# Laying out the on-chip memory of a fused attention and expert kernel anew, and splitting the products of its last layer by halves

## The chip, the cores and the metric

The kernel runs on one core of a Trainium2 chip. The metric is the time of one execution on the device in microseconds (us), the median of several runs. The engines of a core work side by side: TensorE (PE) multiplies, VectorE (DVE), ScalarE (ACT) and GpSimd (POOL) work on elements, SyncE (SP) issues the transfers (DMA).

## The reference, cut to what matters

```python
x = attention(q, k, v)                                     # block-causal softmax, 4 x 8 heads of 64
h = np.maximum(np.maximum(x @ w1, x @ w2), x @ w3)         # 2304 tokens, 512 -> 768
x = h @ w_out                                              # 768 -> 512
p = domain_probs / (domain_probs.sum(-1, keepdims=True) + 1e-09)
out = np.zeros((N, D))
for e in range(4):                                         # 512 -> 1024 -> 512
    h = np.maximum(x @ w1[e], 0.0)
    out += p[:, e:e + 1] * (h @ w2[e])
```

The change concerns the loop over the four experts alone.

## The kernel before, in words

**Arithmetic.** Every matrix product is made of fp32r parts: an operand is split into a high part (a cast on ACT) and a low part (the operand less its high part, a subtraction on DVE), and three matmuls, high by high, high by low and low by high, stand for one. The expert layers add a recursive scheme: the operands are cut into quarters, seven combinations of them (`b11`, `b21`, `t1` to `t4`, `b22`) are multiplied, and sums of the seven products give the four quarters of the result.

**Passes.** The tokens go through the experts in three passes (`NPASS`, line 626; pass 0, 1 and 2 in the code). A pass takes 768 tokens as two columns of `CT` = 384. In pass 0 the second layer is done directly (`second`, line 916, six output tiles of twelve matmuls for each half of an expert). In passes 1 and 2 it is done with the seven combinations (`second_mixed`, line 1043): `sides` (line 963) makes of each combination of the hidden quarters a high and a low part, 768 wide and for each of two halves of the hidden units; `product2` (line 993) multiplies it by the combined weights, twelve matmuls for each of two output halves `d`; and the product is added to running sums `accs`.

**First layer.** `hidden2` (line 855) does the first layer for one of four groups of hidden units: seven products of six matmuls in three PSUM tiles, in the order `b11 t2 t1 b21 t3 b22 t4`, with additions on DVE between them (`plus`), and the hidden quarters written by `put`: in passes 1 and 2 to `hq` tiles (`Mixed`, line 944). Between its products it takes steps of two generators: `between`, the second layer of the expert before (`pend`), and `behind`, which makes the operands of the next pass.

**Weights.** The combined weights of the first layer are kept in DRAM and loaded by `weights_in` (line 812) into a ring of two tiles `w1` (1792 KB each); a load waits until the last product that reads the old tile is done. Pass 1 begins with the expert that pass 0 ended with, so its first two groups use the two tiles that are there (`kept_w`). The combined weights of the second layer (1024 KB each) are loaded by `wide2` (line 984) into a ring of two tiles `w2`.

**Places.** Pass 0 has a pool `p2` (line 1102) with its weights `w2`, `ws`, `raw`, `mix`, its hidden values `hh` and `hl` and temporaries `tmp`. It is closed at line 1158, and so is the pool of the `arena` (line 54; attention's results, and the output sums of pass 0 and the input of pass 1). Pool `p3` (line 1160) takes over their memory for passes 1 and 2: `accs`, `w2`, `hx`, `tmp`, `pb`, `hq`. A tile of `p3` may be written when the readers of what lay there before are done.

**Last expert.** The second layer of the last expert of pass 2 has no work behind it. `second_last` (line 1006) runs the seven combinations in the order `THEN` (line 684), leaves sums that share an accumulator in PSUM, and stores the four output quarters as they are complete.

**Order.** The kernel is written in program order; a scheduler at build time moves instructions of an engine ahead of others by a model of their times, program order being the priority. `keep_in_program_order` takes an instruction out of that: it stays behind what stands before it. In `second_last` every DVE instruction is kept so (`kept`, line 1007).

Of the kernel before, what the change touches and what calls it, by code (L numbers as in the profile page):

```python
# [23 lines left out]
def program(tc, q, k, v, w123, w_out, probs, e_w1, e_w2, out):  # L24
# [27 lines left out]
    wide = ExitStack()  # L52
    big = wide.enter_context(tc.tile_pool(name="big", bufs=1))
# [15 lines left out]
    mp = moe.enter_context(tc.tile_pool(name="moe", bufs=1))  # L69
    hidden = [mp.tile([P, NF, S], F32R, name=x, tag=x) for x in ("hh", "hl")]  # L70
# [668 lines left out]
    def mix():  # L739

        def put(name, src):
            t = tile_in(p3, "hx", [P, 2, 2 * CT], F32R, 4)
# [83 lines left out]
    def weights_out(e, n):  # L826
        w = tile_in(p2, "w2", W2_, F32R, 3)
        s = tile_in(p2, "ws", W2_, F32R)
        raw = tile_in(p2, "raw", [P, 4, QW_], F32)
        nc.sync.dma_start(out=raw, in_=e_w2[e, n])  # L830
        mix_ = tile_in(p2, "mix", [P, 4, QW_], F32)
# [23 lines left out]
    def hidden2(w, xc, pool, put, between, behind, held_back):  # L855
# [8 lines left out]
        def plus(name, x, y):  # L864
            t = put.room(name) if name[0] == "c" else tile_in(pool, "tmp", [P, CT], F32, NTMP)
# [4 lines left out]
        q1 = tile_in(pool, "tmp", [P, CT], F32, NTMP)  # L870
# [18 lines left out]
    class Plain:  # L889
# [11 lines left out]
        def room(self, name):  # L901
            return tile_in(p2, "tmp", [P, CT], F32, NTMP)
# [6 lines left out]
    def paced(it, wait):  # L909
        for _ in range(wait):  # L910
            yield
        for _ in it:
            yield
            yield

    def second(p, e, hs, wo, first_, last):
        for c in range(2):
            for t in range(TPC):
# [5 lines left out]
                for i in range(G):  # L924
# [3 lines left out]
                    nc.tensor.matmul(out=o, lhsT=hh[:, ts], rhs=wh, start=i == 0, stop=False)  # L928
# [34 lines left out]
    def sides(hs, room, less=None):  # L963
        less = less or (lambda out_, x, y, op: nc.vector.tensor_tensor(out_, x, y, op=op))  # L964

        todo = dict(
            b11=(0, ()), b21=(2, ()), t1=(0, (0, 1, 0)), t2=(0, (0, 3, 0)), t3=(1, (1, 3, 1)), b22=(3, ()),
            t4=(0, (0, 2, 0)),
        )
        for name in THEN:  # L970
            n, mix_ = todo[name]
            made = []
            for h in hs:
                if mix_:
                    x, y, z = mix_
                    less(h[:, x], h[:, y], h[:, z], ALU.subtract)
                src = h[:, n].rearrange("x j s -> x (j s)")
                t = room()
                nc.scalar.copy(t[:, 0], src)  # L979
                less(t[:, 1], src, f(t[:, 0]), ALU.subtract)  # L980
                made.append(t)
                yield made

    def wide2(e, name, pool=None, tag="w2"):
        w = tile_in(pool or p3, tag, [P, NPR, 2, QW_], F32R, 2)
# [7 lines left out]
    def product2(o, w, hx, order, d, start, stop):  # L993
        for n, i in enumerate(order):
            wh, wl = (w[:, i, x, d * P:(d + 1) * P] for x in range(2))
            xh, xl = (hx[n // 2][:, x, (n % 2) * CT:(n % 2 + 1) * CT] for x in range(2))
            for m, (a, b) in enumerate(((wh, xh), (wh, xl), (wl, xh))):
                nc.tensor.matmul(  # L998
                    out=o, lhsT=a, rhs=b, start=start and n == 0 and m == 0, stop=stop and n == NPR - 1 and m == 2,
                    skip_group_check=True,  # L1000
                )

    def ring():
        return tile_in(p3, "hx", [P, 2, 2 * CT], F32R, 4)

    def second_last(p, e, hs, order, accs):
        def kept(out_, x, y, op):
            tc.keep_in_program_order(nc.vector.tensor_tensor(out_, x, y, op=op))

        names = iter(FIRST * 2)  # L1010
        prepared = sides(hs, lambda: xc_tile(next(names)).rearrange("x n k s -> x n (k s)"), kept)
        made = [next(prepared) for _ in range(4)][1::2]
# [5 lines left out]
        ends = dict(b21=(0, 0), t3=(1, 1), b22=(0, 1), t4=(1, 0))  # L1018
        q1 = [None, None]
        for n, name in enumerate(THEN):  # L1020
            w = wide2(e, name, *((xp, "w1") if n % 2 == 0 else (p3, "w2")))
            hx = made.pop(0)
            for d in range(2):
                x = next(prepared, None)
                if d and x:
                    made.append(x)
                m, a = ms[d][chain[name]], accs[d]
                product2(m, w, hx, order, d, name in ("b11", "t1", "t2"), name in ("b21", "b22", "t4"))
                if name == "b11":
                    q1[d] = tile_in(p3, "tmp", [P, CT], F32, NTMP)  # L1030
                    nc.scalar.copy(q1[d], m)
                    yield
                    continue
                x = dict(t1="t1", t2="b22", b22="t4").get(name)
                if x:
                    kept(a[x], a[x], q1[d], ALU.add)
                x = into[name]
                kept(a[x], a[x], m, ALU.add)
                if name in ends:
                    store(p, d, *ends[name], a[x])  # L1040
                yield

    def second_mixed(p, e, hs, order, accs, first_, last):
        prepared = sides(hs, ring)
# [217 lines left out]
```

## Time and profile before

| | us |
|---|---|
| median of 3 runs | 1267.93 |
| lowest, highest | 1266.81, 1269.63 |
| the profiled execution, its own time | 1269.37 |
| its span, first to last instruction | 1267.3 |
| PE busy in the span | 1212.8 |
| mean granted TensorE clock | 0.988 |

The profile is of one execution. A time in its rows counts from the span's start. Attention and the two layers after it fill the span to about 520 us, pass 0 of the experts goes on to about 776 us, and passes 1 and 2 to the end. [...]

### The profile page before, as it was taken

The page shows a single profiled execution, that of the slowest core. Times are in us where ns is not written, and L with a number is a line of the kernel's source. Part 1 is how long each engine was busy: PE and PEld are TensorE (multiplying, and loading weights), DVE is VectorE, ACT ScalarE, POOL GpSimd, SP SyncE. Part 2 cuts the span into 40 slices and gives each one's busy share as a digit, 9 for nine tenths or more (in the row PEclk, how much of TensorE's full clock was granted, in tenths as well). Part 3 has the DMA queues.
Part 4 walks back from the last instruction along what each step waited for, and adds up shares of the span by engine and source line. Part 5 has one row for each costly group of instructions (what it writes and reads, how often), then busy time and mean ns, then how long its engine had stood idle before and what let it go on. Part 6 is the DMA issues. An engine that isn't in the chain of part 4 may idle for free.

```text
span 1267.3 us, 19648 instructions
## 1 busy us (share of the span) xinstructions
PE 1212.8 (96%) x7353; PEld 1162.2 (92%) x7353; DVE 938.4 (74%) x1780; ACT 514.9 (41%) x1076; POOL 355.6 (28%) x442
## 2 busy tenths in 40 slices
PE   6789998999999999999999998999999999999997
PEld 5669997999999999989999997999999999999996
DVE  7969899667566644468988894668787887677866
ACT  7876778445444421333434340233322223222221
POOL 4958787454154122333333340000000000000000
PEclk9989999999999999999999999999999999999998
DMA  8655574654533486678888855777887877767653
GB/s 314 239 166 185 171 260 159 190 165 148 158 101 117 143 322 225 235 295 309 319 302 295 314 204 168 276 279 283 349 301 293 306 264 270 271 248 267 230 205 110
DMA packets 82643, 299.67 MB, mean 236 GB/s; under 512 B 8748, under 2 KB 18036, under 8 KB 69492
## 3 DMA queue, kind: packets, MB, share of 16 engines
q1 hardware_dynamic: 82548, 298.42, 66.7%
q8 instruction: 58, 0.95, 0.3%
q14 instruction: 37, 0.30, 0.1%
HBM read 215.26 MB, written 83.14 MB: 235 GB/s over the span
## 4 chain that ended last, share of the span: by engine, by line
PE 81%; DVE 7%; ACT 6%; DMA 2%; issue 2%; POOL 1%; SPq 0%; ACTq 0%; DVEq 0%; POOLq 0%
PE m L846 27%; PE m L492 18%; PE o L998 16%; PE o L928 3%; PE o L929 3%; PE o L930 3%; PE st L181 3%; PE pv L346 2%; PE m L998 2%; PE tt L251 2%; ACT p L202 2%; DVE mn L195 1%; PE pv L305 1%; DMA w<-ka 1%; DVE arena L426 1%
## 5 line engine op out<-in xcount | busy, mean ns | idle before, releaser
L492 PE MATMUL m<-xh,wt 128*128 128x288 f32 x1120 | 236.7, 297 | 2.1 <-DVE mt L530 1.4
L846 PE MATMUL m<-t,w 128*128 128x384 f32 x1152 | 229.5, 338 | 0.0
L998 PE MATMUL o<-hx,w 128*128 128x384 f32 x1176 | 226.0, 337 | 0.0
L998 PEld LDWEIGHTS o<-hx,w 128*128 128x128 f32 x1176 | 208.1, 188 | 0.0
L846 PEld LDWEIGHTS m<-t,w 128*128 128x128 f32 x1152 | 205.1, 189 | 1.9
L492 PEld LDWEIGHTS m<-xh,wt 128*128 128x128 f32 x1120 | 183.1, 188 | 3.3 <-DVE mt L530 1.8
L846 PE MATMUL m<-b,w 128*128 128x384 f32 x864 | 176.8, 339 | 6.2 <-DMA w<-ka 6.2
L979 ACT CAST hx<-hq 128x768 fp32r<-128x768 f32 x98 | 81.6, 837 | 218.7 <-PE o L998 150.0
L492 PE MATMUL m<-xl,wt 128*128 128x288 f32 x560 | 164.8, 294 | 0.0
L846 PEld LDWEIGHTS m<-b,w 128*128 128x128 f32 x864 | 154.3, 189 | 9.4 <-DMA w<-ka 6.5
L964 DVE TENSOR_TENSOR hx<-hq,hx 128x768 fp32r<-128x768 f32 x98 | 93.3, 954 | 39.7 <-ACT hx L979 39.4
L213 POOL TENSOR_SCALAR p<-p,sm 128x128 f32<-128x128 f32 (+1 forms) x144 | 99.4, 706 | 33.6 <-DVE sm L211 27.9
L492 PEld LDWEIGHTS m<-xl,wt 128*128 128x128 f32 x560 | 105.2, 188 | 0.3
L866 DVE TENSOR_TENSOR tmp<-m,tmp 128x384 f32<-128x384 f32 x144 | 77.9, 549 | 24.8 <-PE m L846 24.3
L202 ACT ACTIVATE p<-st,mn 128x128 f32<-128x128 f32 (+3 forms) x144 | 78.7, 558 | 16.1 <-DVE mn L195 15.8
L492 PE MATMUL m<-hh,wo 128*128 128x288 f32 x384 | 81.4, 298 | 2.7 <-ACT arena L541 1.3
L181 PE MATMUL st<-kk,q 128*128 128x128 f32 (+3 forms) x336 | 67.0, 333 | 10.6 <-ACT q L126 5.3
L928 PE MATMUL o<-w,hh 128*128 128x512 f32 x192 | 74.7, 391 | 0.7 <-ACT hh L906 0.5
L929 PE MATMUL o<-w,hh 128*128 128x512 f32 x192 | 74.7, 390 | 0.0
L930 PE MATMUL o<-w,hl 128*128 128x512 f32 x192 | 74.0, 390 | 0.0
L800 POOL TENSOR_TENSOR w<-raw,w 128x512 fp32r<-128x512 f32 x32 | 47.9, 1517 | 89.8 <-ACT w L798 70.8
L866 DVE TENSOR_TENSOR hq<-m,tmp 128x384 f32<-128x384 f32 x96 | 52.7, 553 | 25.0 <-PE m L846 24.4
(153 smaller groups left out, 2076.7 us busy)
## 6 DMA issues: line engine op xcount, KB each, us to landing
w<-kb SPq DMA_DIRECT2D x56, 1024.0 KB, 5.0
w<-ka SPq DMA_DIRECT2D x30, 1792.0 KB, 7.4
ka<-w SPq DMA_DIRECT2D x16, 1792.0 KB, 6.7
wt<-held SPq DMA_DIRECT2D x54, 512.0 KB, 4.1
kb<-ws SPq DMA_DIRECT2D x16, 1024.0 KB, 7.1
kb<-w SPq DMA_DIRECT2D x16, 768.0 KB, 4.6
arena<-in_w SPq DMA_DIRECT2D x18, 512.0 KB, 4.2
wo<-held SPq DMA_DIRECT2D x12, 768.0 KB, 4.5
```

The costliest lines, as they stand in the source:

```text
L181: nc.tensor.matmul(out=st[:, o + c:o + c + n], lhsT=pair[part][:, q0:q0 + P], rhs=pair["kk"][:, x, c:c + n], start=m == 0, stop=m == len(t ...
L202: nc.scalar.activation(x, st[:, o:o + w], ACTF.Exp, bias=mn[:, col:col + 1], scale=-1.0, accum_out=sm[:, col:col + 1],)
L213: nc.gpsimd.tensor_scalar(x, x, sm[:, col:col + 1], 1.0, op0=ALU.mult, op1=ALU.mult)
L492: nc.tensor.matmul(out=out_, lhsT=w, rhs=x, start=m == 0, stop=m == n - 1)
L846: ins = nc.tensor.matmul(out=m, lhsT=a, rhs=b, start=start and n == 0, stop=stop and n == 3 * KH - 1, skip_group_check=True,)
L866: nc.vector.tensor_tensor(t, x, y, op=ALU.add)
L928: nc.tensor.matmul(out=o, lhsT=hh[:, ts], rhs=wh, start=i == 0, stop=False)
L929: nc.tensor.matmul(out=o, lhsT=hh[:, ts], rhs=wl, start=False, stop=False)
L930: nc.tensor.matmul(out=o, lhsT=hl[:, ts], rhs=wh, start=False, stop=i == G - 1)
L964: less = less or (lambda out_, x, y, op: nc.vector.tensor_tensor(out_, x, y, op=op))
L979: nc.scalar.copy(t[:, 0], src)
L998: nc.tensor.matmul(out=o, lhsT=a, rhs=b, start=start and n == 0 and m == 0, stop=stop and n == NPR - 1 and m == 2, skip_group_check=True,)
```

## The change

The diff does four things.

1. The `arena` stays for the whole kernel. The output sums of pass 0 lie in its first half, the input of pass 1 in its second. The `accs` of passes 1 and 2 are now `places` in it (twelve in the first half, two in the second), and so are the second pair of hidden quarters (`hq01`) and one of the share tiles (`pb1`), both in the second half.
2. A pool `pe` lives through all three passes. It has the ring of `tmp`, and two tiles that pass 0 uses for `ws`, `raw` and `mix` and passes 1 and 2 for the first pair of hidden quarters (`hq00`) and a share tile. `hx` becomes four tiles used in turn. In the pool of the stage before (`moe`) the tiles `xf`, `xh`, `xl` now come first.
3. In the first expert of pass 1, the loads for groups 2 and 3 are asked for right after groups 0 and 1; the first matmul of each product and of each output tile of pass 0's last `second` keeps its program order; that `second` runs one step for three products of `hidden2`, and what is left of it after group 1 is run there.
4. `second_last` is rewritten. The operands of the first half of the hidden units are made between the products of the last `hidden2` (`last_sides`). Products are made half by half, the first halves of `b11` and `t1` first. `b11`, `b21`, `b22` and `t4` load into the `w1` ring, `t1` into the place of `t`, and `t2`, `t3` into `w2`. The order is `b11 t1 b21 t2 t3 b22 t4`, and no DVE instruction is kept in program order.

Cut to its core:

```diff
-    wide = ExitStack()
-    big = wide.enter_context(tc.tile_pool(name="big", bufs=1))
+    big = root.enter_context(tc.tile_pool(name="big", bufs=1))
...
-    def paced(it, wait):
+    def paced(it, wait, every=2):
...
-                    nc.tensor.matmul(out=o, lhsT=hh[:, ts], rhs=wh, start=i == 0, stop=False)
+                    ins = nc.tensor.matmul(out=o, lhsT=hh[:, ts], rhs=wh, start=i == 0, stop=False)
+                    if last and i == 0:
+                        tc.keep_in_program_order(ins)
...
+    def half(o, w, hx, i, j, d, start, stop):
+        wh, wl = (w[:, i, x, d * P:(d + 1) * P] for x in range(2))
+        xh, xl = (hx[:, x, j * CT:(j + 1) * CT] for x in range(2))
+        for m, (a, b) in enumerate(((wh, xh), (wh, xl), (wl, xh))):
+            nc.tensor.matmul(
+                out=o, lhsT=a, rhs=b, start=start and m == 0, stop=stop and m == 2, skip_group_check=True,
+            )
+
+    def ring():
+        turn[0] += 1
+        return tile_in(p3, f"hx{turn[0] % 4}", HX, F32R)
+
+    LAST = ("b11", "t1", "b21", "t2", "t3", "b22", "t4")
+
+    def last_sides(h, made):
+        yield
+        for room, name in zip(FIRST, LAST):
+            made[name] = side(h, name, xc_tile(room).rearrange("x n k s -> x n (k s)"))
+            yield
+            yield
...
+        weights("b11", "t1")
+        prepare("b11")
+        prepare("t1")
+        for name in ("b11", "t1"):
             for d in range(2):
+                product(name, d, 0)
+        weights("b21")
+        prepare("b21")
+        for name in ("b11", "t1"):
+            for d in range(2):
+                product(name, d, 1)
+                close(name, d)
+            if name == "b11":
+                weights("t2")
+                prepare("t2")
+        for name, later in zip(LAST[2:], LAST[4:] + (None, None)):
+            if later:
+                weights(later)
+                prepare(later)
+            for d in range(2):
+                for j in range(2):
+                    product(name, d, j)
+                close(name, d)
...
+    first_ = pe.tile([P, 8 * CT], F32, name="part", tag="part")
+    second_ = pe.tile([P, 4 * QW_], F32, name="mix", tag="mix")
+    parts = dict(
+        ws=first_[:, 0:8 * QW_].rearrange("x (n h f) -> x n h f", n=4, h=2).bitcast(F32R),
+        raw=first_[:, 8 * QW_:12 * QW_].rearrange("x (n f) -> x n f", n=4),
+        mix=second_.rearrange("x (n f) -> x n f", n=4),
+        hq00=first_.rearrange("x (n j s) -> x n j s", n=4, j=2),
+        pb0=second_[:, 0:2 * CT].rearrange("x (c s) -> x c s", c=2),
+    )
...
-            pend = paced(second(0, e, hs, wo, e == 0 and g == 0, ends), 2)
+            pend = paced(second(0, e, hs, wo, e == 0 and g == 0, ends), *((3, 3) if ends else (2,)))
...
+    half_ = KD * NT // 2
+    parts["hq01"] = arena[:, half_:half_ + 8 * CT].rearrange("x (n j s) -> x n j s", n=4, j=2)
+    parts["pb1"] = arena[:, half_ + 8 * CT:half_ + 10 * CT].rearrange("x (c s) -> x c s", c=2)
+    places = [arena[:, o:o + CT] for o in (*range(0, 12 * CT, CT), half_ + 10 * CT, half_ + 11 * CT)]
...
-                hidden2(w, xc, p3, Mixed(h, pb, n % 2), pend, following, False)
+                if p == NPASS - 1 and m == E - 1 and n == NPR - 1:
+                    made0 = {}
+                    following = first_half = last_sides(hs[0], made0)
+                hidden2(w, xc, Mixed(h, pb, n % 2), pend, following, p == 1 and m == 0)
                 xc = made or xc
+                if p == 1 and m == 0 and n < 2:
+                    kept_w.append(weights_in(e, order[n + 2]))
+                    if n:
+                        for _ in pend:
+                            pass
```

## Rows read from the trace of the kernel before

**Rows 1.** The page, part 1: busy time of each engine.

```profile
PE 1212.8 (96%) x7353; PEld 1162.2 (92%) x7353; DVE 938.4 (74%) x1780; ACT 514.9 (41%) x1076; POOL 355.6 (28%) x442
```

**Rows 2.** Waits of PE from 519 us: engine, line, waited for; total, times, longest.

```profile
PE m L846 <- DMA w<-ka: 6.2, 1, 6.2
PE m L998 <- DVE at L1008: 5.3, 2, 3.2
PE m L998 <- DVE b L1008: 2.7, 2, 2.5
```

**Rows 3.** Stretches: length, busy by engine (instructions), granted clock, DMA share, GB/s.

```profile
752.00:784.40 32.40, 32.31 (x164) 29.14 (x162) 18.42 (x29) 4.20 (x8) 3.25 (x2) 1.00 0.37 103
784.40:790.50 6.10, 0.00 (x0) 0.00 (x0) 4.09 (x5) 0.00 (x0) 0.00 (x0) 0.92 0.90 350
790.50:796.60 6.10, 6.08 (x19) 6.09 (x20) 0.56 (x1) 0.48 (x1) 0.00 (x0) 0.52 0.99 421
805.00:1205.00 400.00, 400.00 (x2282) 400.00 (x2281) 311.33 (x469) 110.58 (x159) 0.00 (x0) 1.00 0.76 281
```

**Rows 4.** The chain that ended last, 765 to 800 us: start, length, what.

```profile
775.97 7.32 PE m L846 x42
...
783.30 7.17 DMA w<-ka
```

**Rows 5.** Timeline of SP, 745 to 812 us: start, length, what is issued.

```profile
747.89 0.37 SPq L837 DMA_DIRECT2D kb<-ws  x1
...
783.30 1.86 SPq L810 DMA_DIRECT2D w<-ka  x2
```

**Rows 6.** Timeline of DVE, 756 to 785 us.

```profile
758.34 0.54 DVE L907 SCALAR_TENSOR_TENSOR hl<-tmp,hh 128x384 fp32r<-128x384 f32 x1
...
776.67 1.94 DVE L866 TENSOR_TENSOR tmp<-m,tmp 128x384 f32<-128x384 f32 x4
```

**Rows 7.** Timeline of POOL, 744 to 760 us.

```profile
752.28 3.25 POOL L800 TENSOR_TENSOR w<-raw,w 128x512 fp32r<-128x512 f32 x2 [4.42 <-ACT w L798]
```

**Rows 8.** Stretches at the end, columns as in rows 3.

```profile
1207.00:1221.10 14.10, 14.07 (x81) 13.74 (x79) 8.91 (x17) 1.67 (x2) 0.00 (x0) 1.00 0.49 160
1221.10:1223.60 2.50, 0.01 (x1) 0.02 (x1) 2.45 (x4) 0.83 (x1) 0.00 (x0) 0.90 0.89 354
1223.60:1228.20 4.60, 4.60 (x19) 4.60 (x20) 3.40 (x4) 0.03 (x1) 0.00 (x0) 0.69 0.66 239
1228.20:1241.60 13.40, 13.40 (x77) 13.06 (x75) 8.24 (x10) 6.48 (x9) 0.00 (x0) 1.00 0.72 242
1241.60:1248.50 6.90, 1.39 (x4) 0.58 (x3) 5.77 (x9) 0.83 (x1) 0.00 (x0) 0.64 0.12 46
1248.50:1255.20 6.70, 6.70 (x25) 6.70 (x26) 4.67 (x7) 0.83 (x1) 0.00 (x0) 0.60 0.00 0
1263.40:1267.30 3.90, 0.00 (x0) 0.00 (x0) 0.55 (x1) 0.00 (x0) 0.00 (x0) 1.00 0.14 53
```

**Rows 9.** Timeline of the end, 1200 to 1268 us.

```profile
1219.50 0.51 PE L998 MATMUL m<-b,w 128*128 128x384 f32 x2
...
1223.45 1.82 DVE L1008 TENSOR_TENSOR t<-hq,t 128x768 fp32r<-128x768 f32 x2
...
1239.77 0.95 DVE L1008 TENSOR_TENSOR hq<-hq 128x768 f32<-128x768 f32 x1
...
1240.76 0.84 ACT L979 CAST t<-hq 128x768 fp32r<-128x768 f32 x1 [2.36 <-DVE hq L1008]
...
1241.63 0.96 DVE L1008 TENSOR_TENSOR t<-hq,t 128x768 fp32r<-128x768 f32 x1 [0.90 <-ACT t L979]
```

**Rows 10.** Waits of ACT, 805 to 1000 us, columns as in rows 2.

```profile
ACT hx L979 <- DMA xmt<-hx: 7.5, 2, 6.3
```

**Rows 11.** The page, part 6: transfers: count, KB each, median us to landing.

```profile
w<-kb SPq DMA_DIRECT2D x56, 1024.0 KB, 5.0
...
kb<-ws SPq DMA_DIRECT2D x16, 1024.0 KB, 7.1
```

More of the change, by code (lines that the diff above doesn't have):

```diff
@@ L69, in program @@
     mp = moe.enter_context(tc.tile_pool(name="moe", bufs=1))
+    for _ in range(4):
+        mp.tile([P, S], F32, name="xf", tag="xf", bufs=4)
+    for x in ("xh", "xl"):
+        mp.tile([P, KD, S], F32R, name=x, tag=x)
     hidden = [mp.tile([P, NF, S], F32R, name=x, tag=x) for x in ("hh", "hl")]
@@ L853, in multiply, with hidden2 @@
                 n += 1
-    def hidden2(w, xc, pool, put, between, behind, held_back):
+    def hidden2(w, xc, put, between, behind, held_back):
         def product(m, name, start, stop):
@@ L869, in hidden2 @@
         product(m[0], "b11", True, False)
-        q1 = tile_in(pool, "tmp", [P, CT], F32, NTMP)
+        q1 = temp()
         nc.scalar.copy(q1, m[0])
@@ L912, in paced @@
         for _ in it:
-            yield
-            yield
+            for _ in range(every):
+                yield
     def second(p, e, hs, wo, first_, last):
@@ L961, in __call__, with side, sides, wide2 @@
             nc.vector.scalar_tensor_tensor(to, src, 0.0, by, op0=ALU.max, op1=ALU.mult)
[L963 to L969, printed above, removed]
+    mixes = dict(
+        b11=(0, ()), b21=(2, ()), t1=(0, (0, 1, 0)), t2=(0, (0, 3, 0)), t3=(1, (1, 3, 1)), b22=(3, ()),
+        t4=(0, (0, 2, 0)),
+    )
+    def side(h, name, t):
+        n, mix_ = mixes[name]
+        if mix_:
+            x, y, z = mix_
+            nc.vector.tensor_tensor(h[:, x], h[:, y], h[:, z], op=ALU.subtract)
+        src = h[:, n].rearrange("x j s -> x (j s)")
+        nc.scalar.copy(t[:, 0], src)
+        nc.vector.tensor_tensor(t[:, 1], src, f(t[:, 0]), op=ALU.subtract)
+        return t
+    def sides(hs):
         for name in THEN:
-            n, mix_ = todo[name]
             made = []
             for h in hs:
[L974 to L981, printed above, removed]
+                made.append(side(h, name, ring()))
                 yield made
-    def wide2(e, name, pool=None, tag="w2"):
-        w = tile_in(pool or p3, tag, [P, NPR, 2, QW_], F32R, 2)
+    def wide2(e, name, w=None):
+        if w is None:
+            w = tile_in(p3, "w2", W2W, F32R, 2)
         with tc.issue_after(after.pop().ins) if after else nullcontext():
@@ L994, in product2, with second_last @@
         for n, i in enumerate(order):
[L995 to L1001, printed above, removed]
-    def ring():
[L1004 to L1012, printed above, removed]
+            half(o, w, hx[n // 2], i, n % 2, d, start and n == 0, stop and n == NPR - 1)
+    def half(o, w, hx, i, j, d, start, stop):
[5 more added lines that the diff above has]
+            )
+    turn = [0]
+    def ring():
+        turn[0] += 1
[6 more added lines that the diff above has]
+            yield
+            yield
+    def second_last(p, e, hs, order, accs, first_half, made0):
         ms = [
@@ L1018, in second_last @@
         ends = dict(b21=(0, 0), t3=(1, 1), b22=(0, 1), t4=(1, 0))
+        begins, closes = ("b11", "t1", "t2"), ("b21", "b22", "t4")
         q1 = [None, None]
-        for n, name in enumerate(THEN):
-            w = wide2(e, name, *((xp, "w1") if n % 2 == 0 else (p3, "w2")))
-            hx = made.pop(0)
-            for d in range(2):
[L1024 to L1041, printed above, removed]
+        made1, ws = {}, {}
@@ new lines, in weights, with prepare @@
+        def weights(*names):
+            for name in names:
+                if name == "t1":
+                    t = xp.tile(W2W, F32R, name="t", tag="t")
+                elif name in ("t2", "t3"):
+                    t = None
+                else:
+                    t = xp.tile(W2W, F32R, name="w1", tag="w1", bufs=2)
+                ws[name] = wide2(e, name, t)
+        def prepare(name):
+            if name not in made0:
+                next(first_half)
+                next(first_half, None)
+            made1[name] = side(hs[1], name, ring())
@@ new lines, in product, with close @@
+        def product(name, d, j):
+            hx = (made0, made1)[j][name]
+            for n in (2 * j, 2 * j + 1):
+                half(
+                    ms[d][chain[name]], ws[name], hx, order[n], n % 2, d, name in begins and n == 0,
+                    name in closes and n == NPR - 1,
+                )
+        def close(name, d):
+            m, a = ms[d][chain[name]], accs[d]
+            if name == "b11":
+                q1[d] = temp()
+                nc.scalar.copy(q1[d], m)
+                return
+            x = dict(t1="t1", t2="b22", b22="t4").get(name)
+            if x:
+                plus_to(a[x], a[x], q1[d])
+            x = into[name]
+            plus_to(a[x], a[x], m)
+            if name in ends:
+                store(p, d, *ends[name], a[x])
@@ L1202, in program @@
             pend = paced(behind, 0)
-    for _ in second_last(NPASS - 1, e, hs, order, accs):
-        pass
+    second_last(NPASS - 1, e, hs, order, accs, first_half, made0)
     rt.close()
```

51 lines of the change are left out of this document (23 added, 28 removed).

## The prediction

> **What bounds the kernel now.** First the page's busy times: PE is busy 96% of the span, the next engine, DVE, 74% [rows 1]. So time can only come from the gaps of PE and from stretches in which its clock is low. Second the waits of PE after 519 us: the three largest groups are 6.2, 5.3 and 2.7 us [rows 2]. Third the table of stretches, which says where they lie. Between 805 and 1205 us PE is busy 400 of 400 us [rows 3], so the middle of passes 1 and 2 has nothing to give. One gap lies where pass 0 hands over to pass 1 (784.4 to 790.5), three lie in the last expert's second layer (1221.1 to 1248.5) [rows 3, 8]. Behind both, the granted clock falls: 0.52 in 790.5 to 796.6, 0.69, 0.64 and 0.60 in three stretches of the end [rows 3, 8].
>
> **What the handover costs now.** The chain of waits runs from PE's 42 matmuls at 775.97 into the load of `w1` at 783.30, which takes 7.17 us [rows 4]. Why so late? DVE finishes pass 0's hidden values at 758.9, and its next write to a `tmp` is at 776.67, after the last output tile [rows 6]: `tmp` and `hq` of pool `p3` lie over `hh` and `hl`. Without a copy of `b11` in `tmp`, `hidden2` stops after three products. So groups 0 and 1 of pass 1 finish at 784.4, and only then do their two `w1` tiles come free; both loads are issued within 1.86 us from 783.30 [rows 5]. Idle: 6.2 us. Half clock: 19 matmuls in 6.1 us are 0.32 each, against 77 in 13.40, 0.174 each, at full clock [rows 3, 8]; 19 x 0.146 = 2.8 us. Together 9.0 us.
>
> **What the change makes of it.** `tmp` lives in `pe` and waits for nothing. `hq00` lies over `ws` and `raw`. Their last readers are a transfer issued at 747.89, 7.1 us to landing, so 755.0, and POOL until 755.5 [rows 5, 7, 11]. The first write to `hq00` follows four products (six matmuls, 1.05 us each) begun at 752, so at 756.2 or later: free, with 0.7 us to spare. PE has 32.3 us of work from 752 to 784.4 [rows 3]: 14 products of groups 0 and 1 and one left over (15.7), and six output tiles, 2.8 each. In the new order group 0 ends after eight products and one tile, at 763.2; its load is there at 770.4, and group 2 wants it at 784.4. Group 1 ends two tiles before 784.4, at 778.8; its load lands at 786.0, wanted by group 3 at 791.7. Spare: 14.0 and 5.7 us. On SP the two loads now stand between the six stores of pass 0's output, in order; a store held back there is waited for only by the first write to `places`, some 10 us after the last tile.
>
> What is late next? The kept order takes away the scheduler's fillers in groups 0 to 3. `t4` adds to the tile that DVE reads after `t3`, with one product between (1.05 us): one DVE operation takes 0.54 [rows 6], so a second one in front of it stalls PE. Bounds: 0 and 4 x 0.54 = 2.2 us; I take 0.8, nearer the lower end, since in two of the four groups a tile of 2.8 us stands close by. Gain of the handover: 9.0 - 0.8 = 8.2 us.
>
> **What the end costs now.** From 1221.1 to the last matmul's end at 1263.4 are 42.3 us. The second layer of the last expert has 7 x 2 x 12 = 168 matmuls, of which two ran early [rows 9]: 166 x 0.174 = 28.9 us. Excess: 13.4 us, of which 8.0 are waits for DVE [rows 2] and 5.4 half clock. The cause is DVE's strict order. One combination for one half is a subtraction at 1239.77, a cast on ACT at 1240.76, the low part at 1241.63 until 1242.6 [rows 9]: 2.8 us, in which DVE stands still for 0.9. Two halves take 5.6 us and the sums come on top, while PE needs 24 x 0.174 = 4.2 us for a combination.
>
> **What the change makes of it.** Count of matmuls, weight loads, casts and subtractions: unchanged. Three first halves (`b11`, `t1`, `b21`) are made during the last `hidden2`: 3 casts and 4 DVE operations, 4 x 0.95 = 3.8 us, where DVE now has 14.1 - 8.9 = 5.2 us free [rows 8]. After 1221.1 DVE has 16 operations 768 wide and 13 of 384. Behind one another the former start every 0.87 us (1.82 for two of 0.95 [rows 9]), the latter every 0.47 (1.94 for four [rows 6]): 13.9 + 6.1 = 20.0 us. PE asks for the operands of `t2` 12.5 us after 1221.1, of `t3` 16.7, of `b22` 20.9, of `t4` 24.7; DVE's work up to there is 7.6, 12.0, 15.6 and 20.0. It keeps some 4.7 us ahead everywhere. Loads (5.0 us [rows 11]): `b21` gets its place at 1221.1, lands at 1226.1, is wanted at 1229.4; `b22` lands at 1232.3, wanted at 1242.0; `t4` at 1238.6, wanted at 1245.8. The load of `t1` moves up in SP's queue, into a stretch with the DMA engines 49% busy [rows 8]. The 3.9 us after the last matmul [rows 8] stay.
>
> What is late next is the last `hidden2`: the added DVE operations can stand in front of its sums. Bounds 0 and 2.5 us (one 0.95 before each of its five sums, half covered); I take 1.2. Gain of the end: 13.4 - 1.2 = 12.2 us.
>
> **At nothing** go the moved tiles of the stage before, the sharing of `ws`, `raw` and `mix` in one tile each, and `accs` and `hq` at fixed places: PE covers them, with 32.31 of 32.40 and 400 of 400 us busy [rows 3]. If that cover goes, the price is the third rival's.
>
> **Sum.** 8.2 + 12.2 = 20.4 us. The profiled execution took 1269.37 us, 2.1 more than its span of 1267.3 and 1.4 more than the median of 1267.93. Taken off the median: **1247.5 us**.
>
> [...] Consecutive DVE operations start 0.87 us apart though each takes 0.95 [rows 9]: they overlap. [...]
>
> **The rivals.** *DVE becomes the bound of the end.* If the scheduler leaves DVE standing 0.9 us behind each cast as now, for the nine halves that remain (`b21` one, `t2`, `t3`, `b22`, `t4` two each), DVE needs 20.0 + 8.1 = 28.1 us, 3.4 more than PE leaves. A gap of 2.5 us was followed by half clock here, 19 matmuls in 4.6 us, 1.3 us lost [rows 8]; so 3.4 + 1.5 = 4.9, and 1252.4 us. For it: the chain of cast and subtraction stays. Against: in the middle of the passes, where the same operations are not kept in order, PE never waited [rows 3]. Chance 0.17.
>
> *The handover keeps a wait.* The margin of `hq00` is 0.7 us. If its memory is free late, PE, now held in program order, stands where before it ran ahead to the output tiles. A delay of 3 us, the length of POOL's last pair of operations [rows 7], and half clock behind it of 2.8 us: 1253.3 us. Chance 0.11.
>
> *Slower.* `hx` is now taken strictly in turn, and in pass 1 seven of these tiles are held by transfers that save the next pass's input. One such hold was up to 6.3 us [rows 10]. If each of the seven made PE wait 6.3 less the 2.1 us of a product of the second layer, 7 x 4.2 = 29 us, the result would be 1277. It decides from 2.9 us per hold upwards. Against: now too a ring of four is used, and those holds cost PE nothing [rows 3]. Chance 0.04.
>
> *It does not do what it says*, because waits of the same size come back in another place of the two stretches: 1268, chance 0.04.
>
> **How the numbers follow.** A measurement of this kernel can tell about 0.2%, 2.5 us. Forecast 0.64, rivals 0.17, 0.11, 0.04, 0.04. Faster: 0.64 + 0.17 + 0.11 = 0.92; same 0.04; slower 0.04. The range's low end is the full gain of 22.4 us, 1245.5, less the 1.5 us by which runs differ; the high end takes in both first rivals with the upper bounds of the residues (1253.3 + 2.7): 1244 to 1256.
>
> **What would show it.** Right: no wait of PE for `w<-ka` near 785 us; both loads issued near 763 and 779 us; granted clock 1.00 through both stretches; 168 matmuls of the last expert in about 29.5 us; the span some 20 us shorter and PE's idle time after 752 under 3 us. Wrong: a gap of over 2 us in either stretch with a clock under 1.00 behind it (then look which engine it waited for), or PE no longer busy 400 of 400 us between.

## The result, and the profile after

| | before | after |
|---|---|---|
| median, us | 1268.66 (1266.81 to 1269.63, 4 runs) | 1252.81 (1251.02 to 1254.97, 4 runs) |
| ratio of the medians, 95% interval | | 0.9877 [0.9857, 0.9898] |
| span of the profiled execution, us | 1267.3 | 1251.1 |
| mean granted TensorE clock (1.00 is full speed) | 0.988 | 0.995 |

The changed kernel is 15.85 us faster. Part 1 of the page answers to [rows 1]: the same instructions, and PE busy for 7.1 us less, since the stretches at a clock of 0.52 to 0.69 in the handover and the end [rows 3, 8] stand at 1.00 now (below).

```profile
PE 1205.7 (96%) x7353; PEld 1156.2 (92%) x7353; DVE 935.0 (75%) x1780; ACT 515.5 (41%) x1076; POOL 356.7 (29%) x442
```

The waits of PE from 519 us, columns as in [rows 2]: the 6.2 us for `w<-ka` are gone, and so are both waits for DVE. In their place stands one of 2.1 us for ACT, and one of 1.1 us for a load.

```profile
PE m L848 <- ACT tmp L873: 2.1, 1, 2.1
PE m L1007 <- DMA w<-kb: 1.1, 1, 1.1
PE o L1007 <- DMA w<-kb: 0.5, 1, 0.5
PE o L930 <- ACT hh L908: 0.5, 1, 0.5
PE o L930 <- ACT tmp L1223: 0.2, 1, 0.2
```

Stretches of the kernel after, columns as in [rows 3]. The handover (first three) has its one gap at 758.3, the end (fifth) lost 1.2 us of 30.1, and the clock is 1.00 in every row.

```profile
753.90:788.40 34.50, 32.39 (x164) 29.23 (x163) 20.04 (x29) 3.33 (x8) 3.25 (x2) 1.00 0.49 167
758.30:760.40 2.10, 0.02 (x1) 0.03 (x1) 2.10 (x5) 0.89 (x2) 0.00 (x0) 1.00 0.92 355
760.40:768.00 7.60, 7.60 (x39) 7.05 (x40) 4.55 (x9) 0.00 (x0) 0.00 (x0) 1.00 0.19 64
805.00:1205.00 400.00, 400.00 (x2283) 399.80 (x2282) 309.07 (x471) 109.68 (x158) 0.00 (x0) 1.00 0.76 282
1217.20:1247.30 30.10, 28.87 (x165) 28.16 (x163) 22.50 (x36) 6.51 (x9) 0.00 (x0) 1.00 0.53 186
1247.30:1251.10 3.80, 0.00 (x0) 0.00 (x0) 0.51 (x1) 0.00 (x0) 0.00 (x0) 1.00 0.14 54
```

SP's timeline, answering to [rows 5]: the two loads that were issued together at 783.30 now go out 16 us apart, and group 2 begins at 788.37 without a wait.

```profile
767.59 0.32 SPq L813 DMA_DIRECT2D w<-ka  x1
...
783.45 0.58 SPq L813 DMA_DIRECT2D w<-ka  x1
```

**Where the time came from.** All kernels here have 7353 matmuls, so a trace can be laid beside that of the kernel before by number: the start of the n-th matmul after, less its start before (the median over 13 neighbours; times of the kernel before are told on its own clock). At 745 us of the kernel before this difference is +1.78 us, at 1215 us -4.20, at the last matmul -16.14. So the stages ahead of the handover lost 1.78, the handover gave 5.97 (forecast 8.2), and the end gave 11.94 (forecast 12.2). Forecast were 20.4 us in all; the two large misses are 2.2 us of the handover and 1.8 us ahead of it.

**The gap of 2.1 us at the handover.** Three timelines of the kernel after show it. PE first: after `b11`, `t2` and `t1` of group 0 it waits for a copy (L873, of `b11`'s sum into `q1`) before `b21` may add to the same tile.

```profile
754.98 1.21 PE L848 MATMUL m<-b,w 128*128 128x384 f32 x6
756.02 2.25 PE L848 MATMUL m<-t,w 128*128 128x384 f32 x12
760.38 1.31 PE L848 MATMUL m<-b,w 128*128 128x384 f32 x6 [2.11 <-ACT tmp L873]
```

`b11` is done at 756.2. But on ACT the copy stands behind the last hidden value of pass 0, which waits 3.4 us for DVE:

```profile
759.43 0.52 ACT L908 ACTIVATE hh<-tmp 128x384 fp32r<-128x384 f32 x1 [3.42 <-DVE tmp L868]
759.86 0.46 ACT L873 COPY tmp<-m 128x384 f32<-128x384 f32 x1
```

and DVE comes to that sum (L868) only at 758.86, at the end of a row without a gap:

```profile
752.92 0.94 DVE L673 TENSOR_TENSOR t<-arena,t 128x768 fp32r<-128x768 f32 x1
...
754.25 1.99 DVE L673 TENSOR_TENSOR b<-arena,b 128x768 fp32r<-128x768 f32 x1
756.17 1.64 DVE L909 SCALAR_TENSOR_TENSOR hl<-tmp,hh 128x384 fp32r<-128x384 f32 x1
757.73 0.74 DVE L940 SCALAR_TENSOR_TENSOR arena<-o,prt,arena 128x512 f32<-128x512 f32 x1
758.39 0.54 DVE L909 SCALAR_TENSOR_TENSOR hl<-tmp,hh 128x384 fp32r<-128x384 f32 x1
758.86 0.55 DVE L868 TENSOR_TENSOR tmp<-m,tmp 128x384 f32<-128x384 f32 x1
```

DVE's lateness has a source in the same rows. Its instructions at 754.25 and 756.17 took 1.99 and 1.64 us; the same two forms take 0.94 (first row) and 0.54 us (at 758.39). The two long ones ran beside a pair on POOL:

```profile
754.14 3.25 POOL L803 TENSOR_TENSOR w<-part,w 128x512 fp32r<-128x512 f32 x2 [4.42 <-ACT w L801]
```

Of the 64 instructions of L909 in this trace the 37 with nothing beside them on POOL took 0.54 to 0.56 us, and every longer one (up to 1.65) ran beside POOL. Together the two cost DVE 2.1 us, as much as PE then waited. No run moved POOL's pair, so that the wait would go with it is not shown.

The kernel before had the same late copy, 4.6 us behind its `b11` (done at 753.4):

```profile
757.59 0.53 ACT L906 ACTIVATE hh<-tmp 128x384 fp32r<-128x384 f32 x1 [1.96 <-DVE tmp L866]
758.01 0.46 ACT L871 COPY tmp<-m 128x384 f32<-128x384 f32 x1
...
763.03 0.48 ACT L871 COPY tmp<-m 128x384 f32<-128x384 f32 x1 [4.56 <-PE m L846]
```

There it cost nothing, as PE was busy with output tiles from 756.3 on.

In the rows of the kernel after, ACT does not take the copy, whose product is done at 756.2, ahead of the value that waits until 759.43: the two ran in the order of ACT's queue, the copy at 759.86.

### The profile page after: what moved, and what is told of

Its sections match the earlier page's. It is cut to its first block, busy times and chain, and to the rows that moved or that the text cites. A ratio compares the mean times of both kernels' runs of the same rounds, so it can differ in the third digit from the quotient of the medians.

```text
span 1251.1 us, 19677 instructions
## 1 busy us (share of the span) xinstructions
PE 1205.7 (96%) x7353; PEld 1156.2 (92%) x7353; DVE 935.0 (75%) x1780; ACT 515.5 (41%) x1076; POOL 356.7 (29%) x442
## 4 chain that ended last, share of the span: by engine, by line
PE 66%; DVE 15%; DMA 8%; ACT 6%; issue 3%; POOL 2%; SPq 0%; ACTq 0%; DVEq 0%; POOLq 0%
PE m L848 20%; PE m L495 18%; PE o L1007 17%; DMA t<-in_e_w 4%; PE st L184 3%; PE pv L349 2%; PE tt L254 2%; PE m L1007 2%; ACT p L205 2%; DVE mn L198 1%; DVE hl L909 1%; DVE tmp L868 1%; DVE w L803 1%; DMA w<-kb 1%; DVE arena L940 1%
## 5 line engine op out<-in xcount | busy, mean ns | idle before, releaser
L868 DVE TENSOR_TENSOR tmp<-m,tmp 128x384 f32<-128x384 f32 x144 | 77.8, 549 | 21.3 <-PE m L848 21.0
L978 ACT CAST hx<-hq 128x768 fp32r<-128x768 f32 x49 | 40.6, 836 | 98.9 <-PE o L1007 75.9
L803 POOL TENSOR_TENSOR w<-part,w 128x512 fp32r<-128x512 f32 x32 | 49.0, 1552 | 89.8 <-ACT w L801 70.1
L533 DVE TENSOR_TENSOR mt<-m,mt 128x288 f32<-128x288 f32 x96 | 43.3, 452 | 39.1 <-PE m L495 38.4
L254 PE MATMUL tt<-ident,p 128*128 128x128 f32 x400 | 59.8, 279 | 11.5 <-POOL p L216 7.8
```

The source lines that it names most:

```text
L254: nc.tensor.transpose(tt[:, c:c + P], pt[i][:, k0:k0 + P], ident)
L803: eng.tensor_tensor(w[:, a:b, 1], raw[:, a:b], f(w[:, a:b, 0]), op=ALU.subtract)
```

## The experiments

All ran beside the kernel before, whose median was 1269.34, 1269.32 and 1269.04 us in the three batches; the row "after" is that of the first table, with 1268.66. The three columns on the right are the differences described above: at 745 us, from there to 1215, and from there to the last matmul, each of one profiled execution.

| kernel | median, us | ratio [interval] | to 745 | handover | end |
|---|---|---|---|---|---|
| after | 1252.81 | 0.9877 [0.9857, 0.9898] | +1.78 | -5.97 | -11.94 |
| after_again | 1253.02 | 0.9873 [0.9855, 0.9892] | +2.44 | -6.03 | -12.38 |
| end_only | 1258.13 | 0.9913 [0.9896, 0.9930] | +1.33 | -0.09 | -11.96 |
| hand_only | 1264.88 | 0.9966 [0.9955, 0.9977] | +2.05 | -5.97 | -0.55 |
| dve_free | 1264.01 | 0.9964 [0.9951, 0.9977] | +0.59 | -0.18 | -6.27 |
| half_kept | 1258.61 | 0.9922 [0.9907, 0.9938] | +1.63 | -3.92 | -6.37 |
| no_early | 1252.39 | 0.9865 [0.9850, 0.9880] | +1.03 | -5.91 | -11.89 |
| tile_first | 1250.63 | 0.9853 [0.9838, 0.9868] | +1.79 | -8.71 | -11.87 |
| no_hold | 1250.85 | 0.9857 [0.9843, 0.9872] | +1.23 | -7.91 | -12.39 |
| relu_pool | 1250.59 | 0.9852 [0.9832, 0.9873] | -0.10 | -6.80 | -11.50 |
| load_ahead | 1252.34 | 0.9867 [0.9849, 0.9885] | +0.89 | -4.16 | -12.87 |
| both_mended | 1250.12 | 0.9849 [0.9831, 0.9866] | +1.47 | -7.84 | -12.87 |
| moe_old | 1254.69 | 0.9887 [0.9869, 0.9906] | +2.20 | -4.52 | -12.41 |

### The two halves of the change, each alone

**end_only** is the kernel before with part 4 of the change alone, its `hx`, `tmp` and places as before:

```diff
-    for _ in second_last(NPASS - 1, e, hs, order, accs):
-        pass
+    second_last(NPASS - 1, e, hs, order, accs, first_half, made0)
```

> The kernel before with the new second layer of the last expert alone (places as before). Theory: the two parts of the change are separate, and the end is worth 12.0 us of the trace of after (from the last but one stretch to the end), so 1268.7 - 12 = 1256.7 us; the 6.2 us wait for w1 near 784 us and the half clock behind it stay. Rival: the end's gain needs the new places (fixed hx, sums in the arena), and less than 8 us are left: over 1260.5. Rival: the end gained more than the trace shows because an earlier start of the handover moved loads out of its way: under 1255.

**hand_only** is the kernel after with the `second_last` of before, DVE kept in order and halves together:

```diff
-    second_last(NPASS - 1, e, hs, order, accs, first_half, made0)
+    for _ in second_last(NPASS - 1, e, hs, order, accs):
+        pass
```

> The kernel after with the old second layer of the last expert. Theory: what is left is the handover (5.9 us off) less 1.8 us that the trace of after loses ahead of 752 us: 1268.7 - 4.1 = 1264.6 us, with no wait for w1 near 785 us, a wait of about 2 us of PE for ACT near 758 us, and the waits of 2.5, 2.2 and 3.2 us in the end as before. Rival: the loss ahead of 752 us is chance, then 1262.8 us. Rival: the handover is worth nothing by itself: 1268.7.

Measured: 11.2 and 4.5 us less than the kernel before, 15.7 together against 15.85 of the whole change. Within what runs differ by, some 1.5 us, the parts add up. In end_only the handover stands as it was; its waits of PE still have the row

```profile
PE m L846 <- DMA w<-ka: 6.2, 1, 6.2
```

### What the end gained from: a free order or the rest

The change takes the kept order off DVE in the last second layer, and it does a rest: products half by half, another order of the seven products, other places for their weights. The free order was tried without the rest, and the rest without the free order. **dve_free**, on the kernel before:

```diff
         def kept(out_, x, y, op):
-            tc.keep_in_program_order(nc.vector.tensor_tensor(out_, x, y, op=op))
+            nc.vector.tensor_tensor(out_, x, y, op=op)
```

> The kernel before with the DVE instructions of the last second layer no longer kept in program order; nothing else. It tells whether the end's gain is the freed order or the halves. Theory of the prediction (DVE stands 0.9 us behind each cast because of the strict order): the freed order gives more than half of the end's 12 us, so 1262.5 us or less. Rival: what counts is that operands of the first half exist before the last first-layer product, so the freed order alone gives under 3 us, over 1265.7.

**half_kept**, on the kernel after, keeps every DVE instruction of the last second layer (operands and sums) in program order:

```diff
-            nc.vector.tensor_tensor(h[:, x], h[:, y], h[:, z], op=ALU.subtract)
+            keep(nc.vector.tensor_tensor(h[:, x], h[:, y], h[:, z], op=ALU.subtract))
...
-            plus_to(a[x], a[x], m)
+            tc.keep_in_program_order(nc.vector.tensor_tensor(a[x], a[x], m, op=ALU.add))
```

> The kernel after with every DVE instruction of the last second layer kept in program order, as before the change. Theory of the prediction: DVE then stands still behind the casts again and about half of the end's gain goes, 1252.8 + 6 = 1258.8 us or more, with waits of PE for DVE and a clock below 1.00 in the last 40 us. Rival: the halves and the early operands carry the gain, and the order costs under 2 us: under 1254.8.

Measured at the end: 6.27 us by the free order alone, 6.37 by the rest alone, 11.94 by both. Each gives about half, and neither makes the other superfluous; the time of dve_free lies between its two expectations. The halves were not tried without the new order of products and the new places of the weights, and the longer of the two waits that dve_free leaves is for a load. So what share of the 6.4 us is the halves' own stays open. What each leaves is seen in PE's waits from 1200 us. dve_free:

```profile
PE m L998 <- DMA w<-kb: 2.9, 1, 2.9
PE m L998 <- DVE b L1008: 1.9, 1, 1.9
```

half_kept:

```profile
PE m L1007 <- DVE b L979: 4.2, 1, 4.2
```

and in half_kept's timeline of DVE, which from 1229 to 1237 us stands still for 0.90 us behind a cast of ACT three times (the last two below), as the kernel before did [rows 9]:

```profile
1234.07 0.96 DVE L979 TENSOR_TENSOR t<-hq,t 128x768 fp32r<-128x768 f32 x1 [0.90 <-ACT t L978]
1234.94 0.95 DVE L976 TENSOR_TENSOR hq<-hq 128x768 f32<-128x768 f32 x1
1236.79 0.96 DVE L979 TENSOR_TENSOR hx<-hq,hx 128x768 fp32r<-128x768 f32 x1 [0.90 <-ACT hx L978]
```

The clock falls behind the longest wait of each: from 1239 to 1246 us its mean is 0.84 in dve_free, whose 2.9 us end at 1243.2, and 0.55 in half_kept, whose 4.2 us end at 1239.6. Behind the 1.9 us of dve_free ten matmuls take 2.01 us, against 1.90 for ten at a clock of 1.00 in after_again, so it hardly fell there, and the kernel after has 1.00 throughout. The first rival's mechanism is real, then: it comes back as soon as DVE is held in order.

**no_early** makes the operands of the first half behind the last `hidden2` in program order, not between its products:

```diff
-                    following = first_half = last_sides(hs[0], made0)
+                    first_half = last_sides(hs[0], made0)
+                    next(first_half)
```

> The kernel after with the operands of the first half made behind the last first-layer product instead of between its products. Theory: PE then finds no operand when that product ends, waits about 2.5 us (a cast and a low part, 1.8 us, behind two sums on DVE) with half clock behind it: 1252.8 + 4 = 1256.8 us. Rival: the scheduler moves these operands ahead anyway, as nothing keeps them in order: no change.

Measured: the same time. Its DVE timeline from 1205 to 1224 us has the operations of the kernel after in the same order: the scheduler takes them ahead by itself, as they are no longer kept. Where these lines stand in the code is worth nothing.

### The wait of 2.1 us in the handover

Three kernels take the wait away in different ways. **tile_first** puts the output tiles of pass 0 one product earlier:

```diff
-*((3, 3) if ends else (2,))
+*((2, 3) if ends else (2,))
```

> The kernel after with the first output tile one product earlier (two products of the first layer before it instead of three), so that PE has 2.7 us of work while ACT's copy of b11 is behind DVE's backlog. Theory: the wait near 758 us falls from 2.1 to under 0.6 us, the time by 1.5 us, about 1251.3. Rival: the wait is not ACT's place in the queue but the tile itself (the output tile needs the same late hidden values), and it only moves: no change.

**no_hold** lets the scheduler place PE's products and tiles in the handover:

```diff
-                    if last and i == 0:
-                        tc.keep_in_program_order(ins)
...
-                hidden2(w, xc, Mixed(h, pb, n % 2), pend, following, p == 1 and m == 0)
+                hidden2(w, xc, Mixed(h, pb, n % 2), pend, following, False)
```

> The kernel after with the kept order of PE in the handover taken out (first matmul of each product of the first expert of pass 1, and of each output tile of pass 0's last step). Theory: PE's 2.1 us wait near 758 us is there because PE is held in order behind a copy on ACT; free, it runs ahead to an output tile, the wait goes and the time falls by up to 2 us (1250.8), unless the scheduler puts the output tiles first and the loads of w1 come late again. Rival: the kept order is what makes the loads early; without it PE waits for w1 at about 785 us for 3 us or more with a low clock behind it, 1256 or more.

**relu_pool** leaves PE's order alone and takes the instruction that waits for DVE out of ACT's queue:

```diff
+            if self.final and key == (1, 0):
+                nc.gpsimd.tensor_scalar(h, src, 0.0, None, op0=ALU.max)
+            else:
+                nc.scalar.activation(h, src, ACTF.Relu)
-            nc.scalar.activation(h, src, ACTF.Relu)
```

> The changed kernel with one difference: the last hidden value (the high part of c21) of pass 0's last group is made by POOL instead of ACT, so that nothing that waits for DVE stands ahead of q1's copy in ACT's queue; the order of PE is as in the changed kernel. Theory (b21 waits 2.1 us in the handover because that copy stands in ACT's queue behind an instruction that waits for DVE's backlog): the copy runs within 1 us of the end of b11's product, near 757 us, b21 does not wait, or under 0.4 us, and the time falls by 1.7 to 2.1 us to 1250.9 us. Rival (the copy waits for something else, such as its place or b11's last matmul): b21 still waits 2 us and the time stays at 1252.8 us.

Measured: 1250.6 to 1250.9 us, 2.0 to 2.4 less than the kernel after, and no wait for the copy in any of the three. In tile_first PE has no wait from 740 to 830 us, and is busy for all of the stretch from 740 to 800:

```profile
740.00:800.00 60.00, 60.00 (x307) 54.72 (x306) 44.31 (x66) 13.72 (x23) 6.68 (x5) 1.00 0.62 211
```

Its handover gives 8.71 us of the 9.0 that were there. relu_pool settles the cause of the wait. ACT's copy now runs as soon as `b11` is done (first row, ACT), the value that DVE delays is made on POOL (second), and `b21` follows `t1` without a gap (third and fourth, PE):

```profile
754.34 0.48 ACT L873 COPY tmp<-m 128x384 f32<-128x384 f32 x1 [0.21 <-PE m L848]
```

```profile
757.82 1.81 POOL L909 TENSOR_SCALAR hh<-tmp 128x384 fp32r<-128x384 f32 x1 [2.10 <-DVE tmp L868]
```

```profile
754.14 2.24 PE L848 MATMUL m<-t,w 128*128 128x384 f32 x12
756.23 1.21 PE L848 MATMUL m<-b,w 128*128 128x384 f32 x6
```

POOL takes 1.81 us here for what ACT does in 0.52 in the kernel after. PE waits 0.2 us for it, and later 0.6 and 0.7 us for loads: 1.5 of the 1.9 us by which its handover, 6.80, falls short of tile_first's. That its time came out as expected is, in the profiled execution, luck. The handover gave only 0.8 us more than that of the kernel after; its profiled execution is 2.6 us shorter than that of after_again because it lost nothing ahead of 745 us (-0.10 against +2.44). It shows what the wait hangs on, and the price of the wait is read from tile_first and no_hold: 2.7 and 1.9 us of the handover.

### The wait of 1.1 us at the end

In the kernel after PE waits at 1224.9 for `b21`'s weights. **load_ahead** issues `t3`'s load behind `b21`'s:

```diff
+                if name == "t3":
+                    after.append(loaded["b21"])
                 ws[name] = wide2(e, name, t)
+                loaded[name] = loads[-1]
```

> The changed kernel with one difference: in the last second layer the load of the weights of t3 is issued behind that of b21. Theory (the wait of 1.1 us near 1224 us is there because the 1 MB of t3 goes ahead on the same DMA engines): b21's weights land 5.0 to 5.5 us after their issue, the wait shrinks to 0.3 us or less, 0.8 to 1.1 us gained, 1251.8 us. Rival (place and load of b21 are late by themselves, or two loads share the engines in whatever order): the wait stays over 0.8 us and the time at 1252.8 us.

Measured: `b21`'s load, issued at 1218.8 in the kernel after and 1.8 us behind that of `t3`, took the time in the first row to land; in load_ahead, issued at 1219.75 as the first of the two, the time in the second:

```profile
DMA to landing us min/median/max: 7.1/7.1/7.1
```

```profile
DMA to landing us min/median/max: 4.8/4.8/4.8
```

PE no longer waits there, and the end gives 12.87 us, 0.9 and 0.5 more than in the two profiles of the kernel after (in the second of these the wait at the same place is 0.7 us and is put down to `hx`). The order of the loads is the cause, not the place: in load_ahead `b21`'s load was issued at the same point of the work (that trace runs 0.9 us later there) and landed 2.3 us sooner behind its issue. The medians (1252.34 and 1253.02 of the same batch) are too close to tell apart, and the profiled execution lost more in the handover than it won here (last section).

**both_mended** is tile_first and load_ahead together. 

> The changed kernel with the output tiles of the handover one product earlier and t3's load behind b21's. If the two losses are independent: 2.0 us and 0.9 us less than the changed kernel, 1249.8 us, no wait of PE over 0.6 us between 740 and 1248 us. Rival (the earlier tiles already shift what the load waits for, as nothing but the last matmul counts): same as with the tiles alone, 1250.6 us.

Measured: 1250.12 us; its runs (1249.2 to 1250.64) lie below all of the kernel after in that batch (1250.79 to 1255.82). Its largest wait of PE from 740 us to the end is 0.5 us. Against tile_first's 1250.63 the second edit can't be told by the time. The traces tell it: the end gives 12.87 us, as in load_ahead, and 11.87 in tile_first, which keeps a wait of 1.2 us for `b21`'s weights. So there the two losses are independent, as first expected.

### What was lost ahead of 745 us

**moe_old** takes the lines out that put `xf`, `xh` and `xl` first in the pool of the stage before:

```diff
-    for _ in range(4):
-        mp.tile([P, S], F32, name="xf", tag="xf", bufs=4)
-    for x in ("xh", "xl"):
-        mp.tile([P, KD, S], F32R, name=x, tag=x)
```

> The kernel after without the early places of xf, xh and xl in the pool of the stage before. It tells whether the 1.0 us wait of PE for a load of wo near 515 us, and the rest of the 1.8 us lost ahead of 752 us, belong to the new places. If they do, the wait is gone and the time about 1 us lower. If they are chance of a run (a load that lands later, a clock that falls in another place), the wait shows no rule over the traces of this study. Rival: the early places were what kept pass 0's start free of waits; without them PE waits at 520 to 545 us, and the time is higher.

**after_again** is the kernel after unaltered, for a second trace. 

> The changed kernel once more, unaltered, for a second trace of it. Theory (what cost 1.8 us ahead of the handover, the half clock near 43 us and the wait of 1.0 us for the load of wo near 515 us, varies from execution to execution): the matmuls at 745 us stand between 0.5 and 2.2 us later than in the kernel before, and at least one of the two marks is missing or changed in size. Rival (it belongs to the new places): both marks return, and the matmuls at 745 us stand again 1.7 to 1.9 us later. The wait of 2.1 us for the copy in the handover and the one of 1.1 us for the weights of b21 return in both cases. Median 1252.5 us, between 1251 and 1255.

Measured: moe_old is no faster (1254.69). The wait for `wo` shrinks from 1.0 to 0.2 us, but from 500 to 560 us PE now has

```profile
PE m L844 <- DVE tmp L864: 1.4, 2, 1.2
```

and the first group of experts starts later: its load of `raw` goes out at 519.1, not 516.4. It loses 1.8 us from 505 to 525 us, more than any other profile. So these places do serve, by this one trace. after_again shows both marks again: a clock of 0.76 from 42 to 49 us, as in the kernel after (1.00 in the kernel before), and the wait of 1.0 us for `wo`; the rival on record holds in that, though the 2.44 us at 745 are more than it allowed. But the first mark, 0.76 as well, is in end_only too, whose program is there that of before, and end_only is 1.33 us later at 745, dve_free 0.59. The step from 505 to 525 us is 0.7 to 1.0 us in seven of the ten profiles with the new places, and 0.38, 0.00 and -0.28 in the others; with the places of before it is 0.25 and -0.26. So some 0.7 us may be the places' doing, and the rest lies within what single executions differ by. That is argued from counts and not shown; no run here settles it.

## Why the prediction was right, and where its size was off

The time, 1252.81, lies in the range only by the part that the range had for the rivals: from 1247.5 the residues at their upper bounds reach 1250.2.

- **What bounds the kernel**: right. Behind 519 us no gap stood anywhere else, and 400 of 400 us stay busy in the middle.
- **`tmp` "over `hh` and `hl`"** was misread. By the sizes and the order of the tiles in the two pools of the kernel before, `tmp` of `p3` lies over `ws` and `raw`, and only `hq` over pass 0's `tmp`, `hh` and `hl`. ACT wrote both copies of `b11` into `tmp` at 758.01 and 763.03 (rows above), so it was not for want of them that `hidden2` stopped after three products. What came late were DVE's sums, from 776.67 on. Whether the memory of `hq` or the order chosen at build held them stays open: no run has the new places without the early requests and the new pace. That all of it together removes the wait of 6.2 us for `w<-ka` is shown by hand_only, and that the kept order of PE is not needed for it by no_hold.
- **Handover**, 8.2 forecast, 5.97 measured. The term that was mis-sized is the residue: "`t4` adds to the tile that DVE reads after `t3`", "I take 0.8". Of the 9.0 us 3.0 stayed: 2.1 in the wait for the copy, 0.55 in a wait for a load of the second layer (PE at 795.37), and 0.3 that tile_first leaves too. It looked for what waits for DVE's reads in the new order, and at the queues of DVE and SP; it did not follow ACT's queue past the moved product `b21`. The wait was at another instruction than `t4`. `t4` itself cost nothing: tile_first has the same order of products and no wait.
- **The kept order** "takes away the scheduler's fillers": named in the residue, but priced at `t4` alone. no_hold shows it as a cost of the change itself, 1.9 us of the handover: before, PE ran ahead to output tiles while the copy was late.
- **`hq00`'s memory**: free in time, as worked out. Its first write came at 761.8, in a row of DVE without a gap.
- **The loads**: forecast "near 763 and 779", issued at 767.6 and 783.5. Of these 4.5 us 1.8 were lost ahead of 745 us and 2.1 in the wait for the copy. Spare enough: no wait at 788.4.
- **End**, 12.2 forecast, 11.94 measured. PE waits for DVE nowhere. The residue of 1.2 has the right size and the wrong place: not sums behind added operations in the last `hidden2`, but 1.14 us for `b21`'s weights. Two numbers of that line failed, "gets its place at 1221.1" and "lands at 1226.1"; "wanted at 1229.4" held. Near 1215 us the kernel after is 4.2 us ahead, so its 1224.9, when PE wanted the weights, is 1229.1 there. The scheduler drew 13 matmuls of the last second layer ahead of the end of the last first-layer product (first row below), where the prediction had two; so that product ended, and the place came free, at 1218.8, which is 1223.0 there, 1.9 late; and behind `t3` the load took 7.1 us, not 5.0 [rows 11], and landed at 1225.9, which is 1230.1.

```profile
1217.76 1.04 PE L848 MATMUL m<-t,w 128*128 128x384 f32 x5
...
1226.04 2.32 PE L1007 MATMUL m<-t,w 128*128 128x384 f32 x12 [1.14 <-DMA w<-kb]
```

- **"The cause is DVE's strict order"** was half of it. The free order is worth 6.3 us alone, and the rest of part 4 alone 6.4.
- **Two slips** that nothing rests on: of the times at which PE asks for operands, 12.5, 16.7 and 20.9 count the two early matmuls and 24.7 does not (0.35 us), and the half clock behind the first rival's gap is 1.3 us in one place and 1.5 in the sum.
- **At nothing** stood the moved tiles of the stage before, with rows of later stretches as cover. The stage at 505 to 525 us was not among them; it lost 0.9 us in the first trace, and whether the moved tiles did it is not shown.
- **DVE's operations one behind another**: as priced. In the kernel after three wide ones start 0.87 us apart too (at 1227.72, 1228.59 and 1229.46, 0.95 us each), and PE waits for none of DVE's.
- **Rivals.** The time lies between the prices of the first two, 1252.4 and 1253.3, but neither mechanism happened. DVE did not become the bound. The handover did keep a wait with PE held in order, by ACT's queue and not by memory. No hold of `hx` by a transfer cost PE anything, with 400 of 400 us busy, and the change does what it says.
- **The signs on record.** Met: no wait for `w<-ka` near 785 us, and the clock at 1.00 through both stretches. Not met: PE idled 3.9 us after 752, not under 3, and the span is 16.2 us shorter, not some 20. The sign of being wrong, a gap of over 2 us with a lower clock behind it, came by half: the gap is there, and the clock stayed. In load_ahead and half_kept, which share this handover, it fell to 0.72 from 760 to 766 us (last section).

The sum was 20.4 us, and 15.85 came: 2.2 less in the handover, 0.3 less at the end, 1.8 lost ahead of both (in the traces; the medians differ from them by 0.2).

## What to carry to other kernels

When a step of PE is pinned to its place, follow every engine that must answer before the next pinned step, ACT's queue too: a small copy behind an instruction that waits for a busy engine cost 2 us of an 8 us gain (in the trace before, it was late already and cost nothing), and letting the scheduler run ahead, or moving a filler one step forward, gave it back. Where two remedies aim at one stall, try each alone: here each gave half. And for a load that is wanted soon, look at what goes ahead of it in the same queue, not only at when its place is free: here it landed 7.1 us after its issue behind another load, and 4.8 us after it as the first.

## What had not been expected of the hardware

**The same pause, two clocks.** The wait for the copy in the handover (2.1 to 2.4 us) is in seven profiles. In five the clock stays at 1.00 behind it, and in two (load_ahead, half_kept) it falls, to 0.72 from 760 to 766 us. The handover of these two gives 4.2 and 3.9 us, against 5.9 to 6.0 in four of the five (the fifth, moe_old, lost 1.6 us to a load besides). The rows of load_ahead, and then of after_again, for the same stretches (columns as in [rows 3]):

```profile
756.00:760.00 4.00, 1.72 (x10) 1.40 (x10) 4.00 (x7) 0.89 (x2) 0.67 (x1) 1.00 0.69 264
760.00:766.00 6.00, 6.00 (x23) 5.10 (x22) 2.17 (x5) 0.00 (x0) 0.00 (x0) 0.72 0.06 24
```

```profile
760.00:766.00 6.00, 4.69 (x23) 4.21 (x24) 3.74 (x7) 0.89 (x2) 0.00 (x0) 1.00 0.34 129
766.00:770.00 4.00, 4.00 (x23) 3.73 (x22) 3.14 (x6) 0.00 (x0) 0.00 (x0) 1.00 0.55 123
```

The pause was 2.28 us in the first and 2.38 in the second, so its length alone does not decide. Of profiled executions with the same handover some had this loss and some had not, and two without the pause (tile_first, no_hold) show 1.00 from 749 to 798 us.

**Of two loads in one queue the second landed late.** Of two loads of 1 MB issued 1.8 us apart the first took 4.9 us and the second 7.1 (kernel after), of two issued 0.4 us apart 4.8 and 7.0 (load_ahead). In both pairs the first issued landed as fast as the median load of this size before (5.0 us, [rows 11]).
